# An attention and MLP kernel: one unpacking step of the weights less, float32 attention for the first four jobs, filler matmuls, and a new planned order

## The chip, the core and the metric

The kernel runs on one core of a Trainium2 chip. The metric is device time in microseconds (us) of one launch, weights and inputs starting in device memory and the result ending there. A core has TensorE (PE in the profile, with PEld for its weight loads), VectorE (DVE), ScalarE (ACT), GpSimd (POOL) and SyncE (SP, which here issues nearly all DMA transfers). Each engine works its own list of instructions in order and waits for others by semaphores.

## The reference

Queries are averaged in pairs of rows, then ordinary attention over 1152 keys for 4 batches of 8 heads of width 64, then an MLP of widths 512, 2048, 512 on the 2304 resulting rows. Inputs and outputs are float32.

```python
q_pool = q.reshape(B, H, S // factor, factor, D).mean(axis=3)
scores = scale * np.matmul(q_pool, k.transpose(0, 1, 3, 2))
scores = scores - np.max(scores, axis=-1, keepdims=True)
attn = np.exp(scores)
attn = attn / (np.sum(attn, axis=-1, keepdims=True) + 1e-09)
...
x = attn_out.transpose(0, 2, 1, 3).reshape(B * S, H * D)
h = x @ w_in
g = h * (1.0 / (1.0 + np.exp(-h)))
return g @ w_out
```

## The kernel before

**Jobs.** Heads come in 16 pairs, four to a batch. A job is one pair and one chunk of 128 pooled query rows (or, for the half chunk left over, two pairs); there are 72 jobs, counted here from 0. A job has two sides, one for each head. `scores(j)` (L708, called the S block of job j below) writes both sides into PSUM, in one buffer for each side, so the S block of job j+1 has to wait for both exponentials of job j. The softmax of a side is a row maximum on DVE (L765), a small `nm` (L772) and the exponential on ACT into `p` in float32 with its row sum (L781). Pairs 0 to 3 multiply Q and K in float32, later pairs in float16 halves.

**P times V.** The exponentials `p` are split into a float16 high half (`phl`, a cast, L398 on ACT or L402 on DVE) and a low half (a subtraction, L422 on POOL or DVE). Both halves are turned by DMA transposes (L808) into `pt`, and 27 matmuls a side (L916, out to `po`) multiply them with the halves of V. For one side of jobs 0 to 3 the turn is made on TensorE instead: nine float32 transposes in three groups into PSUM (`pp`, L822), each group evacuated twice, by a cast on ACT (L672) and a subtraction on DVE (L422). DVE scales `po` by the row sums into rows `x` (L988).

**MLP.** When four pairs of a chunk are done, a block of 128 rows goes through the MLP: 192 matmuls with w_in (L1111), tanh on ACT (L1125), a product on DVE (L1132), a cast on ACT and a subtraction on POOL for the halves `g`, and 48 matmuls with w_out (L1206). There are 18 blocks. `px` (L1045) transposes the rows of the first two blocks on TensorE.

**Weights.** They arrive as 64-bit floats, 32 chunks of 512 columns, and are unpacked on the core. For each chunk a cast scales the upper word into a PSUM tile `mm` (L398 on ACT or L404 on DVE), ACT shifts the lower word (L600), and DVE joins the two (L611) and then puts the sign back (L619), two instructions one behind the other. For w_in a scaling by `more` follows. Then come the float16 high half (`w`, L398) and the low half (L422).

**What sets the order.** The program is not written in its order: a planner (`Plan.order`) walks through modelled time, and on each engine picks the ready operation with the lowest priority number, given the room in tile pools, a modelled cost for each operation and a port that DVE and POOL share. Where an operation can go to two engines, it chooses one. The result is a fixed list for each engine. The numbers in `PRI`, `FIRST_LEAD`, `W_FIRST` and their like shift priorities. Through `early=`, the casts and subtractions of the first eight jobs, of the first four pairs and of the weights were kept off DVE. One PSUM pool, `mm`, has two buffers, and `t` of the weights, `pp`, `po`, `px` and the MLP's products all take their turn in them.

## Time and profile before

| | before |
|---|---|
| median of three runs | 723.63 us (722.24 to 724.0) |
| the profiled execution's own time | 726.18 us |
| its span, first to last instruction | 724.4 us |
| TensorE busy in the span | 652.5 us (90%) |
| ACT, DVE, POOL busy | 495.6, 472.4, 470.7 us |
| mean granted TensorE clock, share of full speed | 0.978 |

The span is cut at the start of S blocks, which both kernels have in the same number and order: job 2, job 8 and job 20. A stretch in which TensorE is busy from end to end is bounded by TensorE; in the others one looks for what the S block waited for. A matmul group that takes twice its usual time runs at the lower of the two clock levels, 1.2 instead of 2.4 GHz.

### The profile page before, as it was taken

To read this page: it belongs to the slowest core of one execution; us is meant where nothing else is said; L and a number is where in the kernel's file an instruction comes from. 1 tells how busy PE (TensorE), PEld (TensorE's weight loads), DVE (VectorE), ACT (ScalarE), POOL (GpSimd) and SP (SyncE) were. 2 spreads that over 40 slices of the span, in tenths; PEclk is the share of its full clock that TensorE was granted. 3 is DMA by queue.
4 is the path that set the end of the run, shared out by engine and by line. 5 is a ranking of instruction groups with operands and counts; after the bars stand their busy time and mean duration, and the time that the engine had idled before them with its cause. 6 is when DMAs were issued, how large, how long until landed. Compare 5 with 4: busy or idle time off the path is not lost.

```text
span 724.4 us, 23311 instructions
## 1 busy us (share of the span) xinstructions
PE 652.5 (90%) x10052; PEld 470.8 (65%) x10052; DVE 472.4 (65%) x852; ACT 495.6 (68%) x722; POOL 470.7 (65%) x264
## 2 busy tenths in 40 slices
PE   4544877979899999998999999999999999999997
PEld 2333555656758685857585858585758585858767
DVE  3888987977867765775875656477697565754110
ACT  4998897897658676775766767675766675765221
POOL 3536886888657676667647877868547676767111
PEclk8798899999999999999999999999999999999999
DMA  8999889999999999999999999999999998999000
GB/s 345 334 306 216 131 158 226 232 193 206 204 320 189 191 164 179 175 224 184 238 208 198 161 185 165 173 243 191 242 208 182 172 176 160 165 166 161 24 15 16
DMA packets 362888, 138.11 MB, mean 191 GB/s; under 512 B 350112, under 2 KB 350368, under 8 KB 362784
## 3 DMA queue, kind: packets, MB, share of 16 engines
q1 hardware_dynamic: 362624, 136.49, 100.0%
q8 instruction: 78, 1.28, 0.7%
q14 instruction: 26, 0.21, 0.1%
q10 hardware_dynamic: 160, 0.13, 0.1%
HBM read 45.09 MB, written 4.72 MB: 69 GB/s over the span
## 4 chain that ended last, share of the span: by engine, by line
PE 57%; DMA 12%; POOL 9%; DVE 8%; ACT 6%; issue 6%; SPq 1%; POOLq 0%; ACTq 0%; DVEq 0%
PE mm L1111 18%; PE mm L1206 17%; PE S L708 11%; PE po L916 10%; DMA pt<-phl 9%; POOL phl L422 4%; DVE nm L765 4%; POOL w L422 2%; ACT p L781 2%; DMA ld<-v 2%; POOL g L422 2%; ACT phl L398 2%; PE mm L1159 1%; SPq L808 1%; DVE mm L611 1%
## 5 line engine op out<-in xcount | busy, mean ns | idle before, releaser
L422 POOL TENSOR_TENSOR phl<-p,phl 128x1152 f16<-128x1152 f32 x121 | 292.6, 2424 | 125.4 <-ACT phl L398 71.6
L781 ACT ACTIVATE p<-S,nm 128x1152 f32<-128x1152 f32 x144 | 175.0, 1216 | 97.9 <-DVE nm L772 52.1
L765 DVE TENSOR_REDUCE nm<-S 128x1 f32<-128x1152 f32 x144 | 194.6, 1351 | 53.5 <-PE S L708 53.4
L1111 PE MATMUL mm<-xt,w 128*128 128x128 f16 x3456 | 204.4, 220 | 7.0 <-DVE t L1132 4.3
L1111 PEld LDWEIGHTS <-w 128*128 128x128 f16 x3456 | 196.7, 98 | 12.4 <-issue 7.4
L1206 PE MATMUL mm<-w,g 128*128 128x512 f16 x816 | 186.5, 379 | 2.0 <-DVE t L1132 1.4
L916 PE MATMUL po<-V,pt 128*128 128x64 f16 (+1 forms) x4320 | 132.0, 195 | 24.5 <-DMA pt<-phl 12.7
L708 PE MATMUL S<-K,Q 64*128 64x512 f16 (+7 forms) x1320 | 136.3, 369 | 13.7 <-ACT p L781 7.3
L916 PEld LDWEIGHTS <-pt 128*128 128x128 f16 (+1 forms) x4320 | 123.1, 101 | 37.9 <-DMA pt<-phl 16.0
L422 POOL TENSOR_TENSOR g<-t,g 128x512 f16<-128x512 f32 x72 | 96.1, 1337 | 69.6 <-ACT g L398 67.9
L398 ACT ACTIVATE phl<-p 128x1152 f16<-128x1152 f32 x115 | 132.2, 1160 | 9.1 <-DMA pt<-phl 5.9
L1206 PEld LDWEIGHTS <-g 128*128 128x128 f16 x816 | 75.8, 98 | 86.1 <-issue 2.6
L1132 DVE SCALAR_TENSOR_TENSOR t<-t,mm 128x512 f32<-128x512 f32 x72 | 49.4, 686 | 68.8 <-ACT t L1125 68.1
L708 PEld LDWEIGHTS <-Q 64*128 64x128 f16 (+1 forms) x1080 | 42.0, 96 | 50.1 <-issue 9.3
L398 ACT ACTIVATE g<-t 128x512 f16<-128x512 f32 x72 | 45.2, 627 | 21.9 <-DVE t L1132 21.6
L1125 ACT ACTIVATE t<-mm 128x512 f32<-128x512 f32 x72 | 42.5, 590 | 25.4 <-PE mm L1111 25.1
L743 DVE TENSOR_SCALAR r<-sum 128x1 f32<-128x1 f32 (+1 forms) x152 | 17.2, 148 | 52.2 <-ACT p L781 51.7
L708 PEld LDWEIGHTS S<-K,Q 64*128 64x128 f32 (+1 forms) x240 | 22.3, 204 | 39.5 <-issue 22.9
L988 DVE TENSOR_TENSOR x<-po,r 128x128 f32<-128x128 f32 x72 | 20.7, 287 | 21.0 <-PE po L916 18.6
L422 POOL TENSOR_TENSOR xs<-x,xs 128x512 f16<-128x512 f32 (+1 forms) x18 | 22.5, 1248 | 16.6 <-ACT xs L398 16.5
L422 DVE TENSOR_TENSOR phl<-p,phl 128x1152 f16<-128x1152 f32 x19 | 28.3, 1495 | 5.8 <-ACT phl L398 4.9
L525 DVE SCALAR_TENSOR_TENSOR V<-ld,V 128x1152 f16<-128x1152 f32 x16 | 21.9, 1373 | 13.5 <-ACT V L398 13.4
(53 smaller groups left out, 415.2 us busy)
## 6 DMA issues: line engine op xcount, KB each, us to landing
ld<-q SPq DMA_DIRECT2D x16, 576.0 KB, 5.2
ld<-v SPq DMA_DIRECT2D x16, 576.0 KB, 6.1
ld<-k SPq DMA_DIRECT2D x12, 576.0 KB, 6.6
pt<-phl SPq DMA_TRANSPOSE x280, 4.4
wide<-w_in SPq DMA_DIRECT2D x8, 512.0 KB, 7.3
wide<-w_out SPq DMA_DIRECT2D x8, 512.0 KB, 8.1
raw<-w_in SPq DMA_DIRECT2D x8, 512.0 KB, 5.8
raw<-w_out SPq DMA_DIRECT2D x8, 512.0 KB, 5.4
```

The lines of the kernel that those rows point to most:

```text
L398: nc.scalar.activation(out=out(), in_=src(), func=AF.Copy, scale=scale or 1.0)
L422: return lambda: getattr(engine, op)(out=out(), in0=a(), in1=b())
L525: lambda: nc.vector.scalar_tensor_tensor(out=values(1), in0=v3(), scalar=V_SCALE, in1=values(0)[:, :, :D], op0=ALU.mult, op1=ALU.subtract,),
L708: nc.tensor.matmul(o[to, c], lhsT=a[rows, s], rhs=x[rows, c], start=n == 0, stop=n == len(terms) - 1,)
L765: lambda: nc.vector.tensor_reduce(out=nm(), in_=ps()[:, :S], op=ALU.max, axis=AX.X),
L781: lambda: nc.scalar.activation(out=p32(), in_=ps()[:, :S], func=AF.Exp, scale=0.0625, bias=nm(), **({} if SUM_BY_PE else dict(accum_out=sm ...
L916: nc.tensor.matmul(o[to, keep : keep + n], lhsT=pt[:, hl * NK + c, cols], rhs=vv[:, at : at + n], start=c == 0 and hl + vl == 0, stop=c == ...
L988: lambda: nc.vector.tensor_tensor(out=to(), in0=sides2()[:, :, :D], in1=r().unsqueeze(2).to_broadcast([P, 2, D]), op=ALU.mult,),
L1111: nc.tensor.matmul(o, lhsT=w[:, f // 2 % 4, wl, cols], rhs=moving(xl, kk), start=kk == 0 and wl + xl == 0, stop=kk == 3 and wl == 1,)
L1125: lambda: nc.scalar.activation(out=t(), in_=h(), func=AF.Tanh, scale=1.0 / G_SCALE),
L1132: lambda: nc.vector.scalar_tensor_tensor(out=t(), in0=t(), scalar=1.0, in1=h(), op0=ALU.add, op1=ALU.mult,),
L1206: nc.tensor.matmul(o(), lhsT=g[ff // 4]()[:, gl, ff % 4], rhs=w[:, u % 4, wl, e * DM : e * DM + DM], start=ff == ffs[0] and gl + wl == 0, ...
```

## The change

Five things change.

- **Sign.** The first scaling of a weight chunk uses a parametric ReLU on ACT, always on ACT, whose slope for negative numbers carries the sign bit through the following shift. So DVE's second instruction (L619) is gone, and the join writes the value directly. The lower word's shift may now run on DVE as well as on ACT, the scaling by `more` and the high half on POOL too.
- **Float32 for the first four jobs.** `SIDES32 = 8`: all eight sides of jobs 0 to 3 are turned on TensorE (`whole`, `pp`), evacuated once as float32, and multiplied with V in float32, nine matmuls a side. No cast, no subtraction and no DMA transpose is left there; the row sums absorb the scale of V. The float16 halves of V for the first four pairs are needed only from job 4 on.
- **Filler matmuls.** `spin` offers up to 60 groups of four matmuls of 256 columns, which read a constant and whose result nobody reads. The planner puts them where its model of TensorE has time and the clock is not safely up; 28 groups are in the program.
- **Restrictions and clock in the planner.** `early=` is gone, so DVE takes casts and subtractions everywhere. The planner's clock is now a model of activity, not a fixed time.
- **All priorities and lead times have new values,** with separate ones for the first eight jobs (`PRE`) and for the stages of weights (`W`) and MLP (`EV`).

```diff
-EARLY, KL_EARLY, T_EARLY, WLO_EARLY, ADD_EARLY = 8, 2, False, True, True
-MLP_EVAC, T_EVAC = 9.35, -2973.437
+SOON = 8
...
-BOTH_BY_PE, ONE_BY_PE, EVERY = 0, 4, 99
+BOTH_BY_PE, ONE_BY_PE, EVERY = 0, 0, 99
...
-EARLY_BY = "act", "dve"
-W_BY = "act", "dve"
+W_BY = "act", "dve", "pool"
+MORE_BY = "act", "dve", "pool"
+LOW_BY = "act", "dve"
...
-SIDES32 = 0
+SIDES32 = 8
...
-            either(
-                cast(512, t, value, 2.0**-111, fast=False),
-                pr, [("raw", *tok)], [("t", *tok)], [t, raw], port=False, early=T_EARLY,
-            )
...
+            add(
+                "act", act_cost(512, True) + 0.06,
+                lambda: nc.scalar.activation(
+                    out=t(), in_=value(), func=AF.Prelu, scale=2.0**-111, alpha=-(2.0**32)
+                ),
+                pr + W["t"], [("raw", *tok)], [("t", *tok)], [t, raw], port=False,
+            )
...
+            def low_on(engine):
+                return lambda: engine.tensor_scalar(
+                    out=words(0).bitcast(U32), in0=words(0).bitcast(U32), scalar1=29, scalar2=None,
+                    op0=ALU.logical_shift_right,
+                )
...
                 lambda: nc.vector.scalar_tensor_tensor(
-                    out=tu(), in0=tu(), scalar=3, in1=words(0).bitcast(U32),
+                    out=words(1).bitcast(U32), in0=tu(), scalar=3, in1=words(0).bitcast(U32),
                     op0=ALU.logical_shift_left, op1=ALU.bitwise_or,
                 ),
-                T_EVAC, [("low", *tok)], [("t", *tok)], [t, raw], port=False,
-            )
-            add(
-                "dve", slow,
-                lambda: nc.vector.scalar_tensor_tensor(
-                    out=words(1).bitcast(U32), in0=words(1).bitcast(U32), scalar=0x80000000,
-                    in1=tu(), op0=ALU.bitwise_and, op1=ALU.bitwise_or,
-                ),
-                T_EVAC, [("t", *tok)], [("raw", *tok)], [t, raw], port=False,
+                pr + W["put"], [("low", *tok), ("t", *tok)], [("raw", *tok)], [t, raw], port=False,
             )
...
             either(
-                cast(S, lambda: phl()[:, 0], p32, by=EARLY_BY if j < EARLY else EITHER),
-                at + PRI["hi"], [("p32", j, i)], [("phi", j, i)], [p32, phl], early=j < EARLY,
+                cast(S, lambda: phl()[:, 0], p32, by=EITHER),
+                at + pri(j, "hi"), [("p32", j, i)], [("phi", j, i)], [p32, phl],
             )
...
+        def spin(n):
+            ps = tile("psM", "mm", [P, 512], F32, "spin")
+
+            def matmuls():
+                x = one().bitcast(F16)
+                for _ in range(4):
+                    nc.tensor.matmul(ps()[:, :256], lhsT=x[:, :P], rhs=x, start=True, stop=True)
+
+            add("pe", 4 * pe_cost(256), matmuls, 1e8 + n, [("one",)], [], [ps, one], matmuls=4, spare=True)
+
+        for n in range(SPARE):
+            spin(n)
```

What the planner makes of it shows at three places. In the rows, names are tiles with a number at their end, `a<-b` is written from read.

**SP's list at its start.** Before, from the seventh transfer on, the loads of q, K and v of pair 2 and, behind the first weights, of pair 3:

```order
L464 DMA ld_99<-q 128x1152
L464 DMA K_101<-k 128x1152
L464 DMA ld_105<-v 128x1152
L585 DMA wide_107<-w_in 128x1024 x2
L585 DMA wide_107<-w_out 128x1024
L464 DMA ld_124<-q 128x1152
L464 DMA K_130<-k 128x1152
L464 DMA ld_140<-v 128x1152
```

Now, from the seventh transfer on, seven weight transfers and then pair 2:

```order
L597 DMA wide_114<-w_in 128x1024 x2
L597 DMA wide_114<-w_out 128x1024 x2
L597 DMA wide_166<-w_in 128x1024 x2
L597 DMA wide_166<-w_out 128x1024
L476 DMA ld_201<-q 128x1152
L476 DMA K_220<-k 128x1152
L476 DMA ld_234<-v 128x1152
```

The load of pair 2's q moves from the 7th to the 14th place on SP. The first DMA transpose moves from the 18th place, as SP's list counts single transfers, to the 37th.

**ACT between the exponentials of job 1 and job 2.** Before, from job 1's second exponential (`p_48`), with `phl` the high half of P and `V` that of V:

```order
L781 ACTIVATE p_48_228,sum_212<-S_32_166,nm_209 128x1152
L672 ACTIVATE pt_237<-pp_223 128x512
L398 ACTIVATE phl_245<-p_48_228 128x1152
L672 ACTIVATE pt_237<-pp_232 128x512
L398 ACTIVATE w_0_58_262<-wide_107 128x512
L600 ACTIVATE wide_107<-wide_107 128x512
L398 ACTIVATE mm_266<-wide_107 128x512
L600 ACTIVATE wide_174<-wide_174 128x512 x2
L398 ACTIVATE V_276<-ld_140 128x1152
```

Now, from job 1's second exponential (`p_63`), with `pt` the evacuated float32 transposes and `mm` a weight chunk's scaling:

```order
L802 ACTIVATE p_63_320,sum_288<-S_40_224,nm_273 128x1152
L410 ACTIVATE w_0_66_331<-wide_114 128x512
L689 ACTIVATE pt_341<-pp_323 128x512
L608 ACTIVATE mm_348<-wide_114 128x512
L689 ACTIVATE pt_341<-pp_343 128x512
L689 ACTIVATE pt_341<-pp_355 128x128
```

The cast of P and of V and the shifts of lower words have left ACT here; evacuations and scalings have come.

**DVE late, between the maxima of job 30 and of job 31.** Before, from the maximum of the first side of job 30:

```order
L765 TENSOR_REDUCE nm_4942<-S_595_4889 128x1
L772 TENSOR_SCALAR nm_4942<-nm_4942 128x1
L988 TENSOR_TENSOR x_572_4690<-po_4914,r_4723 128x2x64
L765 TENSOR_REDUCE nm_4993<-S_594_4888 128x1
L772 TENSOR_SCALAR nm_4993<-nm_4993 128x1
L743 TENSOR_SCALAR r_5079<-sum_4989 128x1 x2
L754 RECIPROCAL r_5079<-r_5079 128x2
L1132 SCALAR_TENSOR_TENSOR t_5065<-t_5065,mm_4975 128x512
L422 TENSOR_TENSOR phl_5083<-p_606_5035,phl_5083 128x1152
L765 TENSOR_REDUCE nm_5140<-S_613_5087 128x1
```

Now, from the maximum of job 30's second side:

```order
L786 TENSOR_REDUCE nm_4927<-S_628_4825 128x1
L793 TENSOR_SCALAR nm_4927<-nm_4927 128x1
L414 CAST phl_4970<-p_636_4941 128x1152
L434 TENSOR_TENSOR phl_4970<-p_636_4941,phl_4970 128x1152
L1153 SCALAR_TENSOR_TENSOR t_5002<-t_5002,mm_4911 128x512
L763 TENSOR_SCALAR r_5028<-sum_4942 128x1 x2
L434 TENSOR_TENSOR phl_5024<-p_639_4972,phl_5024 128x1152
L775 RECIPROCAL r_5028<-r_5028 128x2
L786 TENSOR_REDUCE nm_5093<-S_643_5004 128x1
```

Of the two sides' subtractions (`phl<-p,phl`) one stood on DVE and one on POOL; now both stand on DVE, and a cast with them.

## Rows read from the trace of the kernel before

**Rows 1.** The page: the span, and its part 1, busy time of each engine.

```profile
span 724.4 us, 23311 instructions
...
PE 652.5 (90%) x10052; PEld 470.8 (65%) x10052; DVE 472.4 (65%) x852; ACT 495.6 (68%) x722; POOL 470.7 (65%) x264
```

**Rows 2.** Busy us per engine in five stretches, cut at S blocks; granted clock.

```profile
0.00:29.24 29.24, 12.24 (x41) 7.01 (x41) 15.75 (x26) 18.12 (x27) 12.77 (x13) 0.79 0.98 345
29.24:92.71 63.47, 37.76 (x493) 26.53 (x492) 54.36 (x100) 55.45 (x90) 37.17 (x23) 0.88 0.96 229
92.71:213.53 120.82, 106.45 (x1580) 74.39 (x1581) 94.94 (x170) 97.32 (x144) 92.40 (x57) 0.99 1.09 220
213.53:700.00 486.47, 475.60 (x7672) 343.83 (x7672) 304.20 (x553) 319.47 (x455) 323.76 (x168) 1.00 1.04 178
700.00:724.40 24.40, 20.41 (x274) 19.06 (x271) 3.18 (x5) 5.29 (x9) 4.62 (x4) 0.98 0.08 24
```

**Rows 3.** PE's timeline, merged: start us, length us, operation, count, idle before.

```profile
6.10 4.21 PE L708 MATMUL S<-K,Q 64*128 64x512 f32 x12 [6.10 <-POOL Q L422]
...
16.92 3.96 PE L708 MATMUL S<-K,Q 64*128 64x512 f32 x12
...
29.24 2.92 PE L708 MATMUL S<-K,Q 64*128 64x512 f32 x12
...
73.55 4.21 PE L708 MATMUL S<-K,Q 64*128 64x512 f32 x12
...
92.71 2.21 PE L708 MATMUL S<-K,Q 64*128 64x512 f32 x12 [1.46 <-ACT p L781]
...
118.58 2.84 PE L1111 MATMUL mm<-xt,w 128*128 128x128 f16 x48
...
126.31 4.45 PE L1111 MATMUL mm<-xt,w 128*128 128x128 f16 x48 [2.75 <-DVE t L1132]
...
206.94 6.65 PE L1206 MATMUL mm<-w,g 128*128 128x512 f16 x30
...
213.53 1.64 PE L708 MATMUL S<-K,Q 64*128 64x512 f16 x18
```

**Rows 4.** Groups by line and shape: count, busy us, mean ns, idle before.

```profile
L422 POOL TENSOR_TENSOR phl<-p,phl 128x1152 f16<-128x1152 f32 x121 | 292.6, 2424 | 125.4 <-ACT phl L398 71.6 <-DVE phl L402 44.9 <-DMA pt<-phl 2.9
...
L398 ACT ACTIVATE phl<-p 128x1152 f16<-128x1152 f32 x115 | 132.2, 1160 | 9.1 <-DMA pt<-phl 5.9 <-issue 1.2
...
L422 DVE TENSOR_TENSOR phl<-p,phl 128x1152 f16<-128x1152 f32 x19 | 28.3, 1495 | 5.8 <-ACT phl L398 4.9 <-POOL g L422 0.8
...
L619 DVE SCALAR_TENSOR_TENSOR raw<-raw,mm 128x512 uint32<-128x512 uint32 x16 | 11.1, 694 | 1.0
...
L398 ACT ACTIVATE w<-wide 128x512 f16<-128x512 f32 x16 | 10.7, 666 | 1.5 <-DVE wide L619 1.3
...
L672 ACT ACTIVATE pt<-pp 128x512 f16<-128x512 f32 x8 | 4.7, 599 | 1.3 <-PE pp L822 1.2
...
L398 ACT ACTIVATE mm<-wide 128x512 f32<-128x512 f32 x7 | 4.4, 627 | 0.9 <-DMA wide<-w_in 0.9
...
L672 ACT ACTIVATE pt<-pp 128x128 f16<-128x128 f32 x4 | 1.1, 273 | 0.3 <-PE pp L822 0.3
```

**Rows 5.** POOL's timeline at 23 us, and the page's part 6 on q's loads.

```profile
23.14 1.41 POOL L422 TENSOR_TENSOR Q<-ld 128x576 f32<-128x576 f32 x1 [2.87 <-DMA ld<-q]
...
ld<-q SPq DMA_DIRECT2D x16, 576.0 KB, 5.2
```

**Rows 6.** Timelines at 195 us (POOL, DVE) and 228 us (DVE).

```profile
195.50 1.59 POOL L422 TENSOR_TENSOR xs<-x,xs 128x512 f16<-128x512 f32 x1
196.01 2.31 DVE L422 TENSOR_TENSOR phl<-p,phl 128x1152 f16<-128x1152 f32 x1
...
228.09 1.35 DVE L422 TENSOR_TENSOR phl<-p,phl 128x1152 f16<-128x1152 f32 x1
```

**Rows 7.** PE's waits between 213.53 and 700: total us, times, longest.

```profile
PE po L916 <- DMA pt<-phl: 8.7, 11, 2.1
```

More of the change, by code (lines that the diff above doesn't have):

```diff
@@ L148, in __init__, with add @@
         self.writer, self.readers = {}, {}
[L150 removed]
+    def add(self, options, priority, reads=(), writes=(), tiles=(), port=True, moves=None, matmuls=0, mode=0, spare=False):
         tiles = [x for t in tiles for x in (t, t.share) if x is not None]
[L152 removed]
+        op = Op(options, priority, tiles, port, moves, matmuls, mode, spare)
         before = []
@@ L218, in departs, with windows @@
             return now
+        warm, used, busy, until = False, 0.0, 0.0, WINDOW
+        def windows(now):
+            nonlocal warm, used, until
+            while now >= until:
+                warm = used >= (COOL if warm else HOT) * WINDOW
+                used = min(WINDOW, max(0.0, busy - until))
+                until += WINDOW
         def pick(e, now):
@@ L222, in pick @@
                 op = item[2]
+                if op.spare and warm and used > KEEP * WINDOW:
+                    continue
                 if op.at[e] > now + WAIT or not has_room(op):
@@ L247, in order @@
                 release(op, 0.0)
-        while len(order) < len(self.ops):
+        todo = sum(not op.spare for op in self.ops)
+        while todo:
             if not events:
@@ L316, in order @@
                     order.append(op)
+                    todo -= not op.spare
                     for a in op.after:
@@ L501, in prepare @@
                     rest(NQ, lambda: whole32(qt[p]), q32, lambda: tq()[:, NQ:], ("dve", "pool"), "tensor_add"),
-                    pr, [lq], [("q", p)], [tq, qt[p]], early=first and ADD_EARLY,
+                    pr, [lq], [("q", p)], [tq, qt[p]],
                 )
@@ L630, in weights @@
                 either(
-                    cast(512, value, value, more, by=W_BY),
-                    pr, writes=[("raw", *tok)], tiles=[raw], early=True,
+                    [(e, c + (0.15 if e == "act" else 0.0), f) for e, c, f in cast(512, value, value, more, by=MORE_BY)],
+                    pr + W["more"], writes=[("raw", *tok)], tiles=[raw],
                 )
```

148 lines of the change are left out of this document (77 added, 71 removed).

## The prediction

> **What bounds the kernel now.** I read the page's busy times first: TensorE is busy for 652.5 of 724.4 us [rows 1], so an average of 90%, with 72 us idle. Then the busy times by stretch, cut at the S blocks of jobs 2, 8 and 20 [rows 2]. They show where those 72 us lie: 17.0 before job 2's S block, 25.7 up to job 8's, 14.4 up to job 20's, and 14.9 in the 511 us behind it. Before job 8 the reader is to see that ACT is busy for 55.45 of 63.47 us and DVE for 54.36, while TensorE has only 37.76 us of work there: unpacking the weights and the softmax of the jobs bound it, and the MLP, which is TensorE's large work, cannot start. Between job 8 and job 20 four engines are near each other (106.45, 97.32, 94.94, 92.40 of 120.82). From job 20 on TensorE is the bound, and most of its small idle time is one wait, P times V waiting for the DMA transposes of P (8.7 us) [rows 7].
>
> In the early stretches the granted clock is 0.79 and 0.88 [rows 2]: the S blocks at 6.10, 16.92 and 73.55 take about 4 us, the one at 92.71 takes 2.21 [rows 3]. That is the lower level, after waits of some us. It costs little of the end while ACT is the bound, since it is TensorE's spare time that is spent.
>
> **The comparison I use.** From job 20's S block on, the programs hold the same matmuls, kind by kind (681 and 2880 of the MLP's two large kinds, for one), but for 8 filler matmuls. So the change is worth the time by which job 20's S block starts earlier, plus what the 511 us behind it lose or win.
>
> **Up to job 2.** Before, its S block starts at 29.24 [rows 3]. Now its loads stand later on SP: q of pair 2 is the 14th transfer. Before, the 13th was q of pair 3, behind 6720 KB, and POOL, which waited for it, started at 23.14 [rows 5]. Now 6 loads of 576 KB and 7 weight transfers of 512 KB stand ahead, 7040 KB, so 320 KB more; at 345 GB/s [rows 2] that is 0.95 us, landing at about 24.1. K behind it (576 KB) takes 1.7 us more. So the S block starts at 26, against 29.24; between 24, should the transfers be spread better, and 29.2. The 40 filler matmuls ahead of job 0's S block last, at 0.185 us each by the slow group (4.45 us for 48 of half the columns [rows 3]), at most 7.4 us from about 1.4 us on. They end at 8.8 where Q is ready at 6.10; the S block then runs in 2.21 instead of 4.21 us. So 0.7 us are lost at most, which the load of pair 2 hides.
>
> **From job 2 to job 8.** ACT decides. Between job 1's and job 7's last exponentials its list loses 5 casts of P and one of V (1.16 us each), and 14 shifts, scalings by `more` and high halves of weights (0.666). It gains 6 large and 3 small evacuations (0.599 and 0.273), 15 scalings that were on DVE or come earlier (0.627), and 3 evacuations of the MLP (about 0.6) [rows 4]. The sum is -7.0 - 9.3 + 3.6 + 0.8 + 9.4 + 1.8 = -0.7, so 54.8 of its 55.45 us stay. DVE loses 15 sign instructions (0.694), 10 scalings and 10 subtractions behind `pp`, and gains 5 more joins, 15 shifts or scalings that the trace does not show on DVE (at most the 0.694 of an instruction of that size; below nothing they cannot cost) and 5 casts or subtractions of P; that is within 2 us of nothing. So this stretch doesn't shrink by its work. I leave ACT its 8.0 us of waits (bounds 4 and 14): 62.8 us, and job 8 starts at 88.8, against 92.71. The bounds are 83 and 98.
>
> The 36 added transposes and the float32 products lie in TensorE's 25.7 idle us. By the S block, which does 1152 float32 columns on each half of the array in 2.21 us, nine products of 64 columns are 1.1 us a side, at the lower clock (4.21) 2.1, against 0.8 in float16. For eight sides that is 2 to 10 us more, and without the cover it would cost just that. TensorE also does 24 matmuls of each MLP kind more by then.
>
> **From job 8 to job 20.** TensorE's 106.45 us lose the slow group's excess (4.45 - 2.84 = 1.6), 24 first-layer matmuls (24 x 2.84 / 48 = 1.4) and 24 second-layer ones (24 x 6.65 / 30 = 5.3) [rows 3], and gain one filler group (0.5): 98.6 us. ACT loses 9 casts of P, 12 shifts, scalings or high halves and 5 small MLP steps, and gains 7 scalings and a cast of V, about 15 us of 97. POOL loses 14 subtractions of 2.42, 34 of 92. DVE gains 14 subtractions and 9 casts, loses 20 joins and signs, 12 scalings and some loads' work, and stays near 91. Of four engines near the bound, one is left beside TensorE. The idle time was 14.4; I take 10, between 4 and 18, and job 20 starts at 88.8 + 98.6 + 10 = 197.4, against 213.53. That is 16.1 us earlier; the bounds together give 28 earlier and 1 later.
>
> **Behind job 20.** 58 subtractions of P leave POOL, where one takes 2.42, for DVE, where one takes 1.35 when the port is free (the row at 228.09) [rows 4, 6], and 15 casts leave ACT. DVE goes from 307 to about 398 us, 78% of the stretch; POOL from 328 to 188. What gains is the path from exponential to transpose, by 1.1 us a side, so up to the 8.7 us of TensorE's wait for transposes [rows 7]. What loses is DVE's list, in which maxima, products of the MLP and `po`'s scaling now stand behind these subtractions; each holds a PSUM buffer. I take 2 us lost, between 8 gained and 10 lost.
>
> **The sum.** 197.4 + 510.9 + 2 = 710.3 us of span, 14.1 less than 724.4. The profiled execution took 726.18 (1.8 around its span), 2.55 more than the median of 723.63; the median should go to 709.5.
>
> **Rivals.**
>
> *DVE becomes the bound, and the kernel slower.* A DVE subtraction that starts while POOL reads the same memory waits: at 196.01 it took 2.31 us, POOL's instruction having started at 195.50 [rows 6]. If all 75 behind job 20 did so, DVE would need 75 x 0.96 = 72 us more, 470 of 511. TensorE has MLP work to put between, so I let a third through, 24 us: 733. It eats the gain when 44 of the 75 are held up, that is when their mean passes 1.9 us; it was 1.495 for 19 [rows 4]. Against it speaks that POOL is busy little more than a third of the time now. The Trainium skill (SBUF — State Buffer, Who interferes with whom) says that a VectorE instruction with two SBUF inputs and a GpSimd instruction that reads SBUF lock each other out for the whole instruction, whichever came first keeping the port. The row of 2.31 us agrees, and by that rule moving subtractions to DVE trades POOL's length for DVE's waiting.
>
> *The two `mm` buffers hold back the early jobs.* From job 1's S block (16.92) to job 6's (73.55) 31 tiles pass through them, 2 x 56.6 / 31 = 3.65 us each. Now 60 do, 13 of them fillers (about 0.75 us). At 2.8 us for each of the other 47, (47 x 2.8 + 13 x 0.75) / 2 = 70.7 us, 14.1 more than now, and the gain is gone: 723. For a shorter hold speaks that a transposed group is evacuated once and not twice, and that a weight chunk loses its second join; against it, that ACT's list is full while they wait.
>
> *Everything opens.* Job 8 at 83, 4 us idle up to job 20, and half of the transposes' wait gone: 28 + 4 us earlier, 692.
>
> *The fillers do not lift the clock.* Then the early S blocks stay at 4 us, and by the above ACT still decides; this is inside the forecast.
>
> *The parametric ReLU needs another table.* The program of the change loads one activation table, as before; excluded.
>
> **Chances.** Forecast (700 to 719) 0.58, everything opens 0.12, the two buffers 0.16 (717 to 727), DVE 0.14. A measurement of this kernel tells about 0.3%, 2.2 us, from no change. Faster by more than that: 0.58 + 0.12 + 0.06 of the buffers' case = 0.76; within it 0.10; slower 0.14. The range from 693 to 723 leaves out DVE's case and the ends of two others.
>
> **What would show it.** Job 2's S block near 26, job 8's at 83 to 92, job 20's near 197 in the changed trace; ACT's busy time between jobs 2 and 8 still near 55 us; the DVE subtraction's mean under 1.6 us; TensorE idle for 13 to 18 us behind job 20. Wrong would be job 8 after 95 (buffers), or TensorE waiting behind job 20 for DVE by more than 15 us in total.

## The result, and the profile after

The changed kernel takes 716.02 us (715.03 to 716.72), the kernel before 723.71 on the same chip: a ratio of 0.9894, interval 0.9879 to 0.9909. On another chip, later, it took 713.65 us against 722.16, ratio 0.9885 (0.9844 to 0.9926). Both intervals lie below 1, so it is faster, by 7.7 and 8.5 us, and inside the range; forecast were 14.1. The profiled execution took 716.49 us, its span is 714.7 against 724.4 [rows 1].

The page's part 1, and the busy times by stretch, cut again at the S blocks of jobs 2, 8 and 20 (columns: stretch, length, then busy us and count of PE, PEld, DVE, ACT, POOL, then granted clock, DMA share, GB/s):

```profile
span 714.7 us, 23377 instructions
...
PE 678.1 (95%) x10128; PEld 492.2 (69%) x10128; DVE 553.0 (77%) x903; ACT 464.9 (65%) x691; POOL 304.3 (43%) x204
```

```profile
0.00:27.84 27.84, 22.14 (x148) 16.05 (x148) 15.69 (x30) 15.62 (x26) 9.12 (x13) 0.94 0.94 369
27.84:91.67 63.83, 55.78 (x498) 39.46 (x497) 52.10 (x90) 53.82 (x93) 37.02 (x29) 0.95 0.72 216
91.67:201.57 109.90, 101.72 (x1536) 71.81 (x1537) 95.12 (x157) 84.57 (x126) 67.19 (x43) 0.98 1.13 212
201.57:690.00 488.43, 477.30 (x7666) 345.09 (x7666) 386.90 (x624) 305.00 (x439) 186.37 (x115) 1.00 1.03 180
690.00:714.70 24.70, 21.14 (x287) 19.79 (x284) 3.17 (x5) 5.86 (x10) 4.62 (x4) 0.99 0.08 23
```

Against [rows 2]: job 2 starts 1.4 us earlier. From job 2 to job 8 nothing is gained, 63.83 for 63.47 us, but TensorE is busy in 55.78 of them instead of 37.76. From job 8 to job 20 the stretch is 10.92 us shorter: TensorE has 4.73 us less to do there, and idles 8.2 us instead of 14.4. Behind job 20, 513.1 us stand against 510.9. So the gain is read between jobs 8 and 20, and the early jobs earned part of it: MLP matmuls that stood behind job 8 now run ahead of it, where TensorE had time to spare. By job 8's S block, at 91.67, it has done these MLP matmuls (groups with count, busy us and mean ns):

```profile
L1132 PE MATMUL mm<-xt,w 128*128 128x128 f16 x96 | 5.7, 219 | 0.2 <-DVE nm L793 0.2
L1227 PE MATMUL mm<-w,g 128*128 128x512 f16 x24 | 5.5, 379 | 0.6 <-ACT w L410 0.6
```

Before, by job 8's S block at 92.71, there were 72 of the first kind and none of the second:

```profile
L1111 PE MATMUL mm<-xt,w 128*128 128x128 f16 x72 | 4.5, 219 | 3.3 <-DVE xt L1066 1.7 <-DVE t L1132 1.6
```

That is 24 more of each, as the prediction counted them.

TensorE's timeline around the three cuts, with the float32 product of job 0 ahead of job 2, job 6's S block, and a slow one behind job 8 (start, length, engine, line, out<-in, count, idle before):

```profile
21.15 4.13 PE L925 MATMUL po<-ld,pt 128*128 128x64 f32 x36
...
27.58 0.33 PE L879 MATMUL pp<-one,p 128*128 128x128 f32 x1 [1.26 <-ACT pt L689]
27.84 3.90 PE L725 MATMUL S<-K,Q 64*128 64x512 f32 x12
...
71.78 2.21 PE L725 MATMUL S<-K,Q 64*128 64x512 f32 x12
...
91.67 2.21 PE L725 MATMUL S<-K,Q 64*128 64x512 f32 x12
...
103.02 3.90 PE L725 MATMUL S<-K,Q 64*128 64x512 f32 x12
...
201.57 1.64 PE L725 MATMUL S<-K,Q 64*128 64x512 f16 x18
```

The groups that answer to [rows 4], and TensorE's wait behind job 20 that answers to [rows 7] (total, times, longest):

```profile
L434 DVE TENSOR_TENSOR phl<-p,phl 128x1152 f16<-128x1152 f32 x96 | 145.5, 1522 | 19.0 <-ACT phl L410 15.3 <-issue 0.9 <-DMA pt<-phl 0.8
L434 POOL TENSOR_TENSOR phl<-p,phl 128x1152 f16<-128x1152 f32 x40 | 98.0, 2450 | 55.5 <-ACT phl L410 39.0 <-DVE phl L414 16.5
...
L636 DVE SCALAR_TENSOR_TENSOR raw<-mm,raw 128x512 uint32<-128x512 uint32 x16 | 10.8, 682 | 1.2 <-ACT mm L608 1.1
L621 DVE TENSOR_SCALAR wide<-wide 128x512 uint32<-128x512 uint32 x13 | 5.4, 452 | 0.1
...
L925 PE MATMUL po<-ld,pt 128*128 128x64 f32 x144 | 16.5, 274 | 0.0
L925 PEld LDWEIGHTS po<-ld,pt 128*128 128x128 f32 x144 | 16.4, 192 | 0.0
...
PE po L937 <- DMA pt<-phl: 5.4, 11, 1.1
```

DVE makes 96 subtractions of P instead of 19, at 1.52 us each; the wait for transposes fell from 8.7 to 5.4 us. The eight float32 sides took 16.5 us of TensorE, 2.06 each; their nine matmuls a side stand in the trace as 18 records, each with a weight load.

### The profile page after: what moved, and what is told of

The parts are those of the page before. It is cut to its first block, busy times and chain, and to the rows that moved or that the text cites. A ratio compares the mean times of both kernels' runs of the same rounds, so it can differ in the third digit from the quotient of the medians.

```text
span 714.7 us, 23377 instructions
## 1 busy us (share of the span) xinstructions
PE 678.1 (95%) x10128; PEld 492.2 (69%) x10128; DVE 553.0 (77%) x903; ACT 464.9 (65%) x691; POOL 304.3 (43%) x204
## 4 chain that ended last, share of the span: by engine, by line
PE 37%; DMA 10%; DVE 9%; ACT 6%; issue 3%; SPq 1%; POOL 0%; ACTq 0%; DVEq 0%
PE mm L1132 14%; PE mm L1227 9%; DMA pt<-phl 8%; PE po L937 7%; PE S L725 6%; DVE nm L786 4%; DVE phl L434 3%; ACT phl L410 2%; ACT p L802 2%; DMA ld<-q 2%; PE mm L1180 1%; ACT t L1146 1%; DMA ld<-v 1%; DMA xt<-xs 0%; DVE t L1153 0%
## 5 line engine op out<-in xcount | busy, mean ns | idle before, releaser
L1132 PEld LDWEIGHTS <-w 128*128 128x128 f16 x3456 | 194.7, 98 | 11.4 <-issue 3.8
L434 POOL TENSOR_TENSOR g<-t,g 128x512 f16<-128x512 f32 x71 | 94.0, 1325 | 216.2 <-ACT g L410 187.0
L434 DVE TENSOR_TENSOR phl<-p,phl 128x1152 f16<-128x1152 f32 x96 | 145.5, 1522 | 19.0 <-ACT phl L410 15.3
L937 PE MATMUL po<-V,pt 128*128 128x64 f16 (+1 forms) x4104 | 124.0, 194 | 11.2 <-DMA pt<-phl 6.2
L937 PEld LDWEIGHTS <-pt 128*128 128x128 f16 (+1 forms) x4104 | 115.8, 101 | 23.8 <-issue 8.5
L434 POOL TENSOR_TENSOR phl<-p,phl 128x1152 f16<-128x1152 f32 x40 | 98.0, 2450 | 55.5 <-ACT phl L410 39.0
L410 ACT ACTIVATE phl<-p 128x1152 f16<-128x1152 f32 x85 | 98.3, 1161 | 4.5 <-DMA pt<-phl 2.8
L410 ACT ACTIVATE g<-t 128x512 f16<-128x512 f32 x69 | 43.4, 629 | 20.9 <-DVE t L1153 18.7
L414 DVE CAST phl<-p 128x1152 f16<-128x1152 f32 x51 | 43.0, 842 | 9.0 <-ACT p L802 4.3
L410 ACT ACTIVATE t<-mm 128x512 f32<-128x512 f32 (+1 forms) x16 | 9.2, 578 | 30.9 <-PE mm L1227 21.1
```

The source lines that it names most:

```text
L410: nc.scalar.activation(out=out(), in_=src(), func=AF.Copy, scale=scale or 1.0)
L414: nc.vector.tensor_copy(out=out(), in_=src())
L434: return lambda: getattr(engine, op)(out=out(), in0=a(), in1=b())
L937: nc.tensor.matmul(o[to, keep : keep + n], lhsT=pt[:, hl * NK + c, cols], rhs=vv[:, at : at + n], start=c == 0 and hl + vl == 0, stop=c == ...
L1132: nc.tensor.matmul(o, lhsT=w[:, f // 2 % 4, wl, cols], rhs=moving(xl, kk), start=kk == 0 and wl + xl == 0, stop=kk == 3 and wl == 1,)
```

## The experiments

Three theories of the stretch that bounds the early jobs: **D**, DVE's list holds the pace; **A**, ACT's does; **T**, TensorE's own list does (the float32 products ahead of S). Unless another is named, each kernel keeps every instruction at its place in the changed kernel's order, and only what is named differs. All were timed against the kernel before in the same batch; the interval is the 95% one of the ratio. Starts of S blocks (us):

| kernel | time | ratio to before, interval | job 2 | job 5 | job 8 | job 20 |
|---|---|---|---|---|---|---|
| before | 722 to 723.7 | 1 | 29.24 | 62.76 | 92.71 | 213.53 |
| after | 716.02 | 0.9894 (0.9879 to 0.9909) | 27.84 | 60.09 | 91.67 | 201.57 |
| after, once more | 713.65 | 0.9885 (0.9844 to 0.9926) | 27.47 | 58.59 | 90.24 | 201.13 |
| float16 price | 717.07 | 0.9910 (0.9884 to 0.9937) | 25.46 | 53.83 | 88.40 | 199.96 |
| no fillers | 716.56 | 0.9900 (0.9874 to 0.9926) | 28.63 | 58.57 | 93.67 | 201.18 |
| sign back on DVE | 733.84 | 1.0155 (1.0123 to 1.0187) | 28.91 | 63.39 | 107.48 | 219.38 |
| late subtractions on POOL | 716.87 | 0.9918 (0.9896 to 0.9941) | 27.44 | 58.57 | 90.17 | 199.13 |
| join left out | 709.89 | 0.9824 (0.9792 to 0.9856) | 27.13 | 57.90 | 87.20 | 196.02 |
| early subtractions on POOL | 714.61 | 0.9890 (0.9852 to 0.9928) | 26.59 | 63.81 | 95.90 | 207.35 |
| short unpacking | 714.20 | 0.9892 (0.9861 to 0.9923) | 28.00 | 58.30 | 89.92 | 202.06 |
| float32 undone, planned anew | 747.08 | 1.0321 (1.0281 to 1.0361) | 29.76 | 58.70 | 92.07 | 217.13 |
| before, ReLU alone, planned anew | 753.81 | 1.0429 (1.0389 to 1.0469) | 25.78 | 59.98 | 107.23 | 229.88 |
| before, sign left out | 724.09 | 1.0030 (1.0002 to 1.0057) | 28.56 | 61.01 | 90.83 | 211.16 |
| before, low word left out | 720.05 | 0.9976 (0.9954 to 0.9998) | 28.54 | 59.26 | 88.23 | 214.38 |

The starts are of one execution each. The same program runs in the two rows of after, in "late subtractions on POOL" up to job 20 and in "early subtractions on POOL" up to job 4: it starts job 2 at 26.59 to 27.84, job 5 at 58.57 to 60.09, job 8 at 90.17 to 91.67 and job 20 at 199.13 to 201.57. Differences inside such a spread say nothing. Of each other kernel there is one execution, with a scatter that can be larger: in "early subtractions on POOL", still ahead of its edit, job 3 starts at 42.80, where the other three have it at 37.52 to 39.03.

**The changed kernel once more.**

> The changed kernel itself once more, on the chip of the two others, to see by how much the starts of its S blocks scatter from one execution to the next and to have its time beside theirs. Every theory expects 715 to 717.5 us; job 2 at 26.5 to 28.6, job 8 at 90 to 92.5, job 20 at 199 to 202. A spread beyond that would make the smaller differences of the other runs worthless.

The starts lie within what was expected. The time is 1.4 us under its lower bound; the ratio agrees with the first.

**The float32 products at the price of float16's.**

```diff
-for c in range(NK): matmul(o, lhsT=pt32[c], rhs=v32[c])
+for n in range(3 * NK): matmul(o, lhsT=pt16[n % NK], rhs=one16)
```

> The changed kernel with the same instruction lists, but the products of the first four jobs read P in float16 and a constant in place of V, 27 short matmuls a side as jobs 4 and on have them; so the rows of the first four jobs are wrong, and the time is that of a product at float16's price (about 0.8 us a side; the float32 one took 4.13 us for two sides in the changed kernel's profile). List theory: the product stands in TensorE's list ahead of the transposes and S blocks of the following jobs, and each of jobs 2 to 5 starts 1.5 to 2.5 us earlier; job 6's S block at 63 to 67 instead of 71.8, the median 4 to 8 us lower, 708 to 712. ACT theory (the prediction's): ACT's list decides between job 2 and job 8, TensorE's work there is free; job 8 within 1 us of 91.7 and the median within 1.5 us of 716.

TensorE's timeline of this kernel at job 2:

```profile
19.64 1.74 PE L926 MATMUL po<-one,pt 128*128 128x64 f16 x54
...
25.46 3.85 PE L725 MATMUL S<-K,Q 64*128 64x512 f32 x12
```

Two sides take 1.74 us instead of 4.13, and job 2's S block starts at 25.46, 1.1 to 2.4 us earlier than in the executions of the changed kernel. The lead grows to about 5 us at job 5, is down to 2 or 3 at job 8 and lost in the spread at job 20; the time is no shorter. T is right up to job 5, and job 6's S block, at 65.77, still lies in the 63 to 67 of its forecast. But the time is not in its 708 to 712: the lead pays nothing, and something behind job 5 takes it back.

**No fillers.**

```diff
-for _ in range(4): nc.tensor.matmul(ps()[:, :256], lhsT=x[:, :P], rhs=x)
+pass
```

> The changed kernel with the same instruction lists, but without the 112 filler matmuls. Filler-helps theory: the granted clock before job 8 falls from 0.94 and 0.95 towards the 0.79 and 0.88 of the kernel before, the S blocks of jobs 0 to 7 take about 4 us in four or more cases, and the median is 3 to 8 us higher, 719 to 724. Filler-costs theory: fillers wait for a PSUM buffer in front of needed work (TensorE stood idle 11.7 us ahead of fillers for DVE's instructions in the changed kernel's profile, one time 3.5 us); without them jobs 7 to 9 start 2 to 5 us earlier and the median is 1 to 5 us lower, 711 to 715. The prediction's view: neither, within 2 us of 716, since ACT decides.

Without the fillers, and then with them, in the first profile of the changed kernel:

```profile
6.10 3.87 PE L725 MATMUL S<-K,Q 64*128 64x512 f32 x12 [6.10 <-DMA K<-k]
...
15.42 4.21 PE L725 MATMUL S<-K,Q 64*128 64x512 f32 x12
```

```profile
7.17 2.21 PE L725 MATMUL S<-K,Q 64*128 64x512 f32 x12
...
15.01 3.54 PE L725 MATMUL S<-K,Q 64*128 64x512 f32 x12
```

The first S block runs at the lower clock again, 3.87 us for 2.21, and so does the second, 4.21 us, which took 3.54 in the first profile of the changed kernel and 2.21 in its repeat. The granted clock up to job 2 is 0.88 here, against 0.94 and 1.00 in those two. So the fillers lift the clock. Job 8 starts 2.0 us later than in any execution of the changed kernel, job 20 does not, and the time is the same: the fillers neither gain nor cost anything that shows in it. (The idle time ahead of fillers in the first profile is 8.8 us, 6.8 of it for DVE, and not the 11.7 of the expectation.)

**The sign back on DVE.** ACT scales without the sign, and DVE puts it in with a second join.

```diff
-activation(out=t(), in_=value(), func=AF.Prelu, scale=2.0**-111, alpha=-(2.0**32))
+activation(out=t(), in_=value(), func=AF.Copy, scale=2.0**-111)
+scalar_tensor_tensor(out=words(1), in0=words(1), scalar=0x80000000, in1=tu(), op0=and, op1=or)
```

> The changed kernel with the same lists, but each weight chunk's sign is put back by a second DVE instruction behind the join, and the scaling is a plain copy, as in the kernel before: 32 more DVE instructions of about 0.69 us, 22 us, 20 of them before job 8. DVE-near-the-bound theory: DVE's busy time of 52.1 us of 63.8 between jobs 2 and 8 rises to 65, more than the stretch, so job 8 starts 4 to 10 us later and the median is 5 to 12 us higher, 721 to 728. Room theory: DVE waits 12 us in that stretch and takes in most of it; job 8 under 3 us later, the median 716 to 719.

Most of the loss lies between job 5 and job 8. That stretch in the changed kernel, and in this one:

```profile
60.09:91.67 31.58, 25.98 (x289) 16.98 (x288) 28.34 (x43) 26.88 (x43) 21.68 (x18) 0.95 0.64 128
```

```profile
63.39:107.48 44.09, 31.67 (x289) 21.29 (x289) 38.10 (x57) 28.59 (x46) 21.18 (x19) 0.77 0.57 125
```

DVE is busy 9.8 us more, the stretch is 12.5 us longer. By job 20 17.8 us are lost, and as much in the time against the changed kernel's 716.02. The direction is D's, the size lies beyond its 721 to 728: work put on DVE there cost more than its length. Two things besides DVE's time are in it. The granted clock is 0.77 instead of 0.95, and TensorE needs 5.7 us more for the same 289 matmuls. And a weight chunk keeps its `mm` buffer through the second join too: TensorE waits 7.0 us for that instruction in this stretch.

**The subtractions behind job 20 on POOL.**

```diff
-rest(S, phl[1], p32, phl[0])            # by DVE or POOL, as planned
+rest(...) planned alike, issued by nc.gpsimd for j >= 20
```

> The changed kernel with the same lists, but from job 20 on the 75 subtractions of P that the plan gave to DVE are issued by POOL at the same place (2.45 us each there, 1.52 on DVE). Theory that moving them to DVE paid: TensorE's waits for the transposes behind job 20 rise from 5.4 us, the stretch behind job 20 becomes 3 to 15 us longer than its 513 us, median 719 to 731. Theory that it made no difference or cost: the stretch takes 509 to 514 us, median 712 to 717, as the kernel before needed 510.9 with most of them on POOL. The rule that a DVE and a POOL instruction lock each other out is seen in the mean of the DVE subtractions before job 20 and of POOL's.

From job 20 to 690 us DVE is busy for 297 us instead of 387 and POOL for 360 instead of 186, and the time doesn't move. From job 20 to the end it took 514.9 us instead of 513.1; five executions in which nothing behind job 20 was changed (the two of after, float16 price, short unpacking, early subtractions) have 511.4 to 517.0. So moving the subtractions to DVE neither paid nor cost anything that shows. Nor did it shorten TensorE's wait for transposes by much, which is 6.1 us here against 5.4. With both engines reading the same memory DVE's took 1.52 us in the mean in the changed kernel, where 1.35 is one that runs free [rows 6]. The Trainium skill (SBUF — State Buffer, Who interferes with whom) says that a VectorE instruction with two SBUF inputs contends with a GpSimd instruction that reads SBUF, by an exclusive lock. The trace agrees in kind, the longest of the 96 taking 3.42 us; but their median is 1.36, so the wait falls on fewer than half of them.

**The join left out.** The other side of the sign: DVE's one joining instruction is gone.

```diff
-scalar_tensor_tensor(out=words(1), in0=tu(), scalar=3, in1=words(0), op0=shift_left, op1=or)
+pass
```

> The changed kernel with every instruction at its place, but without DVE's one joining instruction of each weight chunk (0.68 us, 18 of them between the S blocks of jobs 2 and 8); the weights are therefore wrong, and this run prices DVE's time alone, the other way round from the run with the sign put back. Theory D, DVE sets the pace from job 5 to job 12 in the changed kernel: 12.3 us of its 52.1 in that stretch are gone, ACT (53.8) is next; job 2 stays at 27.8 within 0.5, job 8 starts 4 to 8 us earlier than 91.67 and job 20 5 to 12 us earlier than 201.57, the time is 704 to 712. Rival A, ACT's list or TensorE's own sets it and putting the sign back only made DVE late beyond that: job 8 at 90 to 92, job 20 at 199 to 202, 714 to 717. If job 20 comes earlier but the time does not follow, the gain is given back behind job 20.

This kernel is 4 to 6 us faster than the changed kernel, as D had it. Its stretch from job 5 to job 8:

```profile
57.90:87.20 29.30, 25.52 (x290) 16.96 (x289) 24.04 (x32) 26.29 (x43) 21.43 (x18) 0.94 0.73 135
```

DVE lost 4.3 us (28.34 to 24.04), the stretch only 2.3; ACT is busy for 26.29 of what is left. So D is right in the sign, and its size is not borne out here; that ACT then takes over is likely, and not tested.

The edit also takes away what the next step on the same chunk waited for, and lets go of the chunk's `mm` buffer earlier, so it doesn't price DVE's time alone. The next run tried to.

**Short unpacking.** No shift of the low word, and the join becomes a plain shift.

```diff
-low: tensor_scalar(words(0) >> 29) on DVE, or the same step on ACT
-scalar_tensor_tensor(out=words(1), in0=tu(), scalar=3, in1=words(0), op0=shift_left, op1=or)
+tensor_scalar(out=words(1), in0=tu(), scalar1=3, op0=shift_left)
```

> The changed kernel with every instruction at its place, but a weight chunk is unpacked without the lowest 3 of its 23 mantissa bits: the shift of the low word (0.43 us on DVE, about 0.6 on ACT) is left out, and the join (0.68) becomes a plain shift by 3 (0.45 by the other shift of this size). The output is a little less exact. Between the S blocks of jobs 2 and 8 this takes 18 x 0.23 + 11 x 0.43 = 8.9 us from DVE and about 4.4 from ACT. Theory D, the stretch is bound by DVE with ACT and TensorE close behind it: job 8 starts 3 to 7 us earlier than in the repeat of the changed kernel, job 20 5 to 9 us, the time is 705 to 711, about that of the run without the join (709.9). Rival, TensorE's own list holds the stretch by now (55.8 of 63.8 us): job 8 less than 2 us earlier, 712 to 716.

There is no gain: time and job 8 lie where the rival, T, had them. The first group is this run's join, the others the changed kernel's in its repeat, both between 27.5 and 90 us.

```profile
L636 DVE TENSOR_SCALAR wide<-mm 128x512 uint32<-128x512 uint32 x13 | 8.7, 685 | 4.6 <-ACT mm L608 4.6
```

```profile
L636 DVE SCALAR_TENSOR_TENSOR wide<-mm,wide 128x512 uint32<-128x512 uint32 x12 | 8.0, 684 | 1.9 <-ACT mm L608 1.9
...
L621 DVE TENSOR_SCALAR wide<-wide 128x512 uint32<-128x512 uint32 x7 | 2.7, 433 | 0.0
```

My 0.45 for the shift was wrong: out of PSUM it takes 0.685, as the join did. What DVE lost were its other shifts, and in the changed kernel's order all of those stand ahead of job 5. From job 2's S block to job 8's DVE is busy 3.7 us less than in the repeat and ACT 3.5 less, and the stretch is 0.9 us shorter. From job 5's to job 8's, not one DVE instruction became shorter, and that stretch took 31.62 us in this run and 31.65 in the repeat. So this run says nothing on D there. Here are DVE's list and TensorE's in the repeat, a part of that stretch:

```profile
70.60 1.01 DVE L434 TENSOR_TENSOR w<-wide,w 128x512 f16<-128x512 f32 x1
71.54 1.35 DVE L434 TENSOR_TENSOR phl<-p,phl 128x1152 f16<-128x1152 f32 x1
72.81 0.68 DVE L636 SCALAR_TENSOR_TENSOR raw<-mm,raw 128x512 uint32<-128x512 uint32 x1
73.41 1.34 DVE L786 TENSOR_REDUCE nm<-S 128x1 f32<-128x1152 f32 x1
74.67 0.68 DVE L636 SCALAR_TENSOR_TENSOR raw<-mm,raw 128x512 uint32<-128x512 uint32 x1
75.27 0.14 DVE L793 TENSOR_SCALAR nm<-nm 128x1 f32<-128x1 f32 x1
75.33 1.34 DVE L786 TENSOR_REDUCE nm<-S 128x1 f32<-128x1152 f32 x1
...
78.13 1.36 DVE L434 TENSOR_TENSOR phl<-p,phl 128x1152 f16<-128x1152 f32 x1
79.41 0.68 DVE L636 SCALAR_TENSOR_TENSOR raw<-mm,raw 128x512 uint32<-128x512 uint32 x1
```

```profile
68.62 1.74 PE L937 MATMUL po<-V,pt 128*128 128x64 f16 x54 [1.62 <-DVE wide L636]
...
80.14 1.19 PE L1277 MATMUL spin<-one 128*128 128x256 f16 x8 [1.90 <-DVE raw L636]
...
84.95 1.73 PE L937 MATMUL po<-V,pt 128*128 128x64 f16 x54 [1.48 <-DVE raw L636]
```

In the part shown DVE goes from one instruction to the next without a gap (in the whole stretch it idles 3.2 of 31.65 us), and TensorE waits for its joins, 5.0 of the 7.3 us that it idles there: `po` and the filler matmuls need one of the two `mm` buffers, and `t` holds one until DVE has joined it. That fits D from job 5 on, and would explain why relief ahead of job 5 gains nothing. It fits the prediction's rival of the two `mm` buffers as well, since it is the same wait; no run gives the pool a third buffer.

**The early subtractions on POOL.**

```diff
+sub_on_pool if 4 <= j < 12 else as planned
```

> The changed kernel with every instruction at its place, but the DVE subtractions behind the casts of P of jobs 4 to 11 (6 of them, 1.35 us each on DVE, 4 by job 8) issued by POOL, which takes about 2.4 us for each. Theory D, DVE sets the pace here: job 8 starts 2 to 4 us earlier, job 20 2 to 5, and the time is 711 to 715. Rival P, the longer subtraction on the path to the transpose and POOL's weight halves queued behind it cost as much as DVE gains: job 8 within 1.5 us of 91.67, job 20 within 2 of 201.57, 714.5 to 718. If ACT is the bound, the same as rival P for the time, but with DVE's idle time in jobs 5 to 8 grown by 5 us.

The time is that of the changed kernel; 714.61 lies in D's range and in P's. The profiled execution was this kernel's longest (720.42), with job 3 late at 42.80 ahead of any edit: the float32 product ahead of it ran at the lower clock, 7.78 us for 4.13. So of its starts only their distances count. The stretch from job 5 to job 8, in the repeat and in this run:

```profile
58.59:90.24 31.65, 24.38 (x290) 16.34 (x289) 28.45 (x43) 26.88 (x43) 21.73 (x18) 1.00 0.64 124
```

```profile
63.81:95.90 32.09, 25.88 (x290) 16.96 (x289) 23.58 (x40) 26.74 (x43) 28.56 (x22) 0.95 0.57 108
```

DVE is busy 4.9 us less, and the stretch is no shorter. D had 2 to 4 us there, so DVE's load as such does not hold this stretch alone. Whether POOL's longer subtractions cost what DVE gained (P), or ACT's list holds the pace, both of which leave DVE idle for 8.5 us instead of 3.2, the run can't tell.

**Float32 undone, and planned anew.**

```diff
-BOTH_BY_PE, ONE_BY_PE, EVERY = 0, 0, 99
+BOTH_BY_PE, ONE_BY_PE, EVERY = 0, 4, 99
-SIDES32 = 8
+SIDES32 = 0
```

> The changed kernel without float32 in the first four jobs: their second side goes through TensorE's transposes into two float16 halves and their first through the DMA transposes, as in the kernel before (the two constants that say so set back, all other numbers kept), and the order planned anew. Theory D, the float32 way takes load from DVE and ACT in jobs 0 to 4 (four casts and subtractions, six evacuations into low halves) but that load lies before the stretch where DVE is full: job 8 at 91 to 96, job 20 at 201 to 206, the time 715 to 721, so most of the gain of 7.6 us stays. Rival F, float32 is what opens the early jobs: job 8 after 97, job 20 after 208, 722 to 728, the gain is gone.

The time lies far outside both ranges. Job 8 comes at 92.07, close to the changed kernel, so in this order the early jobs reach it without float32; then 15 us are lost by job 20 and 16 more behind it (there TensorE is busy 11 us longer, with 18 MLP matmuls and 16 fillers more among others). The order is a new one, made with numbers fitted to another program, and its price is not separated from that of the part.

**The parametric ReLU alone, in the kernel before, and planned anew.**

```diff
-either(cast(512, t, value, 2.0**-111, ...))          # by ACT or DVE
+activation(out=t(), in_=value(), func=AF.Prelu, scale=2.0**-111, alpha=-(2.0**32))
-two scalar_tensor_tensor
+one scalar_tensor_tensor(out=words(1), in0=tu(), scalar=3, in1=words(0), ...)
```

> The kernel before with the parametric ReLU alone: all 64 chunks scaled by ACT with the sign's factor, one joining instruction on DVE instead of two, before's own numbers and the order planned anew with them. Between jobs 2 and 8 DVE loses 15 sign instructions of 0.69 us and 11 scalings of 0.69, ACT gains up to 11 scalings of 0.63 unless the planner moves other work to DVE. Theory D, DVE and ACT share the bound, so what leaves DVE opens the stretch: job 8 at 86 to 90, job 20 at 200 to 208, 711 to 719. Rival A, ACT alone bound the stretch before, as the prediction had it: job 8 at 91.5 to 99, job 20 at 210 to 218, 720 to 729.

It is 31 us slower than before, beyond A's range. (The weights are 32 chunks, not the 64 of this expectation and of the next.) TensorE's timeline says where:

```profile
82.86 4.21 PE L703 MATMUL S<-K,Q 64*128 64x512 f32 x12 [19.06 <-ACT p L776]
97.25 3.95 PE L703 MATMUL S<-K,Q 64*128 64x512 f32 x12 [10.19 <-ACT p L776]
```

ACT's list holds 33 weight steps between 60.86 and 81.51 with a single exponential among them, and the next S block waits for the second. Again the new plan is measured together with the part. The next two runs keep before's order.

**Before, without the sign instruction.**

```diff
-scalar_tensor_tensor(out=words(1), in0=words(1), scalar=0x80000000, in1=tu(), op0=and, op1=or)
+pass
```

> The kernel before with every instruction at its place, but without DVE's second join of each weight chunk, the one that puts the sign in (0.69 us, 15 of them between the S blocks of jobs 2 and 8, 64 in all); the weights' signs are therefore wrong. It prices in before's order what the parametric ReLU takes off DVE, without planning anew. Theory A, as the prediction had it, ACT (55.45 of 63.47 us there) decides in the kernel before: job 8 starts at 91 to 94 against 92.71, job 20 at 210 to 215 against 213.53, the time is 719 to 724. Rival D, DVE bounds it too (54.36 of 63.47 there): job 8 starts 4 to 9 us earlier, job 20 4 to 14 earlier, 710 to 719.

**Before, without ACT's step on the low word.**

```diff
-activation(out=words(0), in_=halves(1), func=AF.Copy, scale=2.0**-13, bias=...)
+pass
-scalar_tensor_tensor(out=tu(), in0=tu(), scalar=3, in1=words(0), op0=shift_left, op1=or)
+tensor_scalar(out=tu(), in0=tu(), scalar1=3, op0=shift_left)
```

> The kernel before with every instruction at its place, but without ACT's integer step on the low word of each weight chunk (0.67 us, 19 of them between the S blocks of jobs 2 and 8); DVE's first join stays as a plain shift of the same length, so that the weights lose the lowest 3 of 23 mantissa bits and nothing else changes. It is the counterpart of the run that took the sign instruction off DVE in the same order. Theory A, ACT (55.45 of 63.47 us) decides between jobs 2 and 8 in the kernel before: 12.7 us leave it, DVE and the transposes' DMA come next, so job 8 starts 4 to 9 us earlier than in the run without the sign (90.83) and in the kernel before (92.71), that is at 83 to 88; the time 713 to 720. Rival, neither ACT nor DVE alone holds it but the chain of a job's softmax and its transposes: job 8 at 89.5 to 93, 720 to 724.

The stretches from job 2's S block to job 8's, without the sign and without the low word, and ACT's largest wait, in total, in the second:

```profile
28.56:90.83 62.27, 43.09 (x492) 28.95 (x492) 44.56 (x88) 55.08 (x90) 37.20 (x23) 0.77 0.96 234
```

```profile
28.54:88.23 59.69, 39.87 (x492) 27.70 (x492) 54.15 (x98) 45.47 (x70) 37.21 (x23) 0.83 1.02 245
...
ACT phl L398 <- DMA pt<-phl: 5.3, 4, 2.3
```

Without the sign DVE is busy 9.8 us less [rows 2: 54.36], and the 63.47 us from job 2 to job 8 became 1.2 shorter, inside the spread; the time is 1.9 us longer (ratio 1.0030, 1.0002 to 1.0057). The granted clock was 0.77 in that execution instead of 0.88, and what this took back is not separated. Without the low word ACT is busy 10.0 us less, and the stretch became 3.8 shorter, 59.69. Its start of job 8, 88.23, lies between A's 83 to 88 and the rival's 89.5 to 93. So in the kernel before ACT counts for more than DVE, but loosely: of 10 us less 3.8 are gained. What comes next the run doesn't single out: DVE is busy for 54.15 of 59.69, and ACT itself waits for DMA transposes, 5.3 us in the row above, with a DMA share of 1.02. No run takes load off the DMA queue in before's order, and the change does that as well: no transposes for jobs 0 to 3, and a share of 0.72 instead of 0.96 from job 2 to job 8. Of the 4.5 us at job 8, 1.9 are left in the time; the profiled execution, this kernel's longest at 726.67, has lost them again by job 20.

## Why the prediction was right, and where it was off

The side was right; the time was 6.5 us too low. Of these, 4.4 are terms of the sum (a span of 714.7 against 710.3), and 2.1 are the subtraction of 2.55 for the profiled execution's distance to its median: after's own time was 0.5 from its median, so such a distance is no property of the kernel to carry over.

**Job 2** (forecast 26, came 27.84; 1.84 of the miss). The other executions of the same program have 26.59 to 27.47, so up to 1.3 of that is scatter. The loads were judged well: POOL's work on Q, forecast at 24.1, ran from 24.01 to 25.41.

```profile
24.01 1.40 POOL L434 TENSOR_TENSOR Q<-ld 128x576 f32<-128x576 f32 x1 [1.97 <-DMA ld<-q]
```

What failed is the price of the float32 product: 1.1 us a side, from the S block's columns, against a measured 2.06. That the prediction gives 2.1 for the lower clock is a coincidence; at the lower clock two sides took 7.78 us once, 3.9 each. The product loads new weights for each 64 columns, and those loads run for 16.4 of its 16.5 us: 0.114 us of busy time for each of 144. The page of before has float16 loads of this size, 0.028 us of busy time each, and float32 loads of 64x128 in the S blocks, 0.093 each, from which the price could have been taken (loads overlap, so the rows' means of one are longer):

```profile
L916 PEld LDWEIGHTS <-pt 128*128 128x128 f16 (+1 forms) x4320 | 123.1, 101 | 37.9 <-DMA pt<-phl 16.0
...
L708 PEld LDWEIGHTS S<-K,Q 64*128 64x128 f32 (+1 forms) x240 | 22.3, 204 | 39.5 <-issue 22.9
```

18 loads at 0.093 are 1.7 us a side. The Trainium skill (TensorE: Matmul & The Clock Gate, Weight-path perf modes — Fast Weight Load (FWL) and DoubleRow) says that the quick way of loading weights, in four parallel chunks, is not there for FP32. The ratio of 0.114 to 0.028 agrees in direction; what else differs between the two types no run separates. The second half of the failure is that I let the products lie in idle time, where they stand in TensorE's list ahead of S: with float16's price job 2 came at 25.46. At the end the prediction's cover held all the same: the products cost 9.5 us more than at float16's price (16.5 against eight times 0.87), the upper end of its "2 to 10 us more", and the time with the cheaper price is no shorter.

**From job 2 to job 8** (62.8, came 63.83, and 62.77 in the repeat). The length was right, its reason is not shown. For the kernel before, the two runs in its order bear out that ACT counts for more than DVE, not that it alone decides. For the changed kernel, "ACT decides" doesn't hold as it stands: DVE's joins lie on the path from job 5 to job 8, since putting a second one back costs 12.5 us there and taking the first away gains 2.3. Whether this is DVE's time or the `mm` buffers that wait for it stays open, and no run takes ACT's work away from job 5 on. The busy times were forecast closely, ACT 54.8 against 53.82. For DVE, "within 2 us of nothing" came as 54.36 to 52.10, partly by luck: by the prediction's own counts and before's prices the sum is 1.6 us below nothing only if the 15 shifts or scalings cost 0.694 each and the 5 casts or subtractions are all of the dear kind, and 15.6 below at the other end; measured are 11 shifts at about 0.43 and 7 casts and subtractions. What I missed is that busy times of 54 and 52 in one stretch don't say who bounds a part of it.

**From job 8 to job 20** (108.6, came 109.90): TensorE's busy time 98.6 against 101.72, its idle time 10 against 8.2. This was the core of the forecast and it held: work moved ahead of job 8, and fewer waits behind it. The S block at 103.02 ran 3.9 us instead of 2.2, so 1.7 of the 3.1 us by which the busy time was forecast too low are the clock.

**Behind job 20** (+2, came +2.3): right in sum, and by luck so close: the 2 was a choice between 8 gained and 10 lost, and executions of the same stretch scatter over 5.7 us. The subtractions, which I had both gaining and losing, do neither to an extent that shows.

**The rivals.** DVE as the bound, slower: the tipping point was a mean subtraction of 1.9 us, and it was 1.52; the run with POOL, in which 90 us less on DVE gained nothing, shows that DVE doesn't bound the stretch behind job 20. The two `mm` buffers: the mechanism is there, TensorE waits for buffers that `t` holds, for 5.0 us between jobs 5 and 8 in the repeat. But job 1's to job 6's S block took 56.8 us (15.01 to 71.78), against 56.6 before, and not 70.7. The fillers: they do lift the clock, and it is worth nothing that shows in the time, as the text had it.

**What stays open.** How the 8 us divide among the parts. Putting the sign back on DVE costs 17.8 us in the changed order, and taking it off DVE gains nothing in the old one; the float32 products take 16.5 us of TensorE early, and making them cheaper gains nothing at the end; undoing float32 was tried only with a new plan, and the two together lost 31 us. So the parts were not shown to add up. That the order which uses the room they make is part of the gain follows from this as the likeliest reading; no run tests the new order alone.

No run gives a version that beats the changed kernel by more than the spread; the one that was faster, without the join, doesn't compute the weights.

## What to carry to other kernels

Price an instruction by its dearest half: for the matmul of few columns here that was its weight load, and its type's load has a row of its own. Where two engines are nearly full in a stretch, ask for each part of it which list runs without gaps, and which buffers wait for it. Here work taken away ahead of that part gained nothing, and work added in it cost more than its length; but work moved from there to another busy engine gained nothing either, so a list without gaps is not yet the bound. A part of a change that is worth nothing in the old order can be worth much in the new one, so undo parts with the order kept; a plan made anew with numbers fitted to another program measures the plan as well.

## What was not expected of the hardware

A DVE integer shift of 128x512 took 0.43 us from SBUF to SBUF and 0.685 out of PSUM, no less than a shift and an or with a second operand (0.684). In the float32 product of 128x64 weight loads run for 16.4 of 16.5 us, 0.114 us of busy time each. And twice the clock for the first two S blocks, 2.21 us each in the repeat against 3.87 and 4.21 without fillers, made no difference to the time.
